# Second-layer products as three partial products for all blocks, fewer working buffers, a shorter weight decode, and values split out of a buffer of their own, in a fused attention and rational feed-forward kernel on one core

## The chip, the core and the metric

The kernel runs on one core of one Trainium2 chip, as one program. The metric is the device time of one execution in microseconds (us), as the median of several runs. The core's engines that matter here are TensorE (PE, with its weight loads as a row of its own, PEld), VectorE (DVE), ScalarE (ACT), GpSimd (POOL, which here only issues transfers and a few tiny instructions) and SyncE (SP, which issues transfers and transposes by DMA). Each engine works through its own list of instructions in order; they meet through semaphores.

## The reference, cut to what matters

```python
# q, k, v: (8 batches, 8 heads, 576 positions, 64) float32; tau a scalar; weights arrive as float64
scores = (1/8) * q @ k^T
scores = where(scores >= max(scores) - tau, scores, -1e9)      # per row
attn   = exp(scores - max) / (sum + 1e-9)
x      = (attn @ v), heads side by side                        # 4608 tokens x 512

h = x @ w_in                                                   # 512 -> 2048
g = (a0 + a1 h + a2 h^2 + a3 h^3) / (1 + |b0| |h| + |b1| h^2 + 1e-6)
out = g @ w_out                                                # 2048 -> 512
```

The result is float32. Products of 16-bit parts and products of shortened 32-bit parts are therefore done as several partial products that are summed in PSUM.

## The kernel before, in words

**Attention.** The eight heads of a batch are worked on as four pairs. A unit is one pair and one tile of 128 queries (four tiles, and a rest of 64 queries), so a batch has 20 units and the program 160. A unit makes scores on PE (`f_qk`), their row maximum on DVE (`f_max`, lines 786 and 788), the threshold and the exponential on ACT (`f_pre` 801, `f_sum` 805), and then, from the second batch on, splits the weights into a high and a low fp16 part: high on ACT or DVE (`f_hi`, through the helper `times`, lines 303 and 305), low on DVE (`f_lo`, 827). The parts are transposed by DMA and multiplied on PE with the values V, which are split in the same way (`f_av`, 896). In the first batch the weights stay float32 ("plain") and V is used unsplit.

**Values before.** There are five V buffers. A pair's V is loaded into one (`load_v_ops`, 659 and 663), the unused corners are cleared by two small `MEMSET`s on DVE (683), its largest absolute value is found, and when all four pairs of the batch have theirs, the batch's scale. Then V is split: the high part into a work buffer `u` (`vh`, through `times`), the low part over the raw values (`vl`, 712), and the high part copied behind it (`vc`, 715).

**Feed-forward blocks.** 256 tokens form a chunk, and a block is one chunk and four of the 16 tiles of hidden units (the last block is cut into two halves: 73 blocks in the trace). A block makes layer 1 on PE (`f_g1`, 1013: 48 products), takes h out of PSUM on ACT (`f_h`, 1022), and then runs a chain over 128x1024 tiles: |h| on ACT or DVE, four multiply-adds on DVE for the two polynomials (1033, 1036, 1046 and, after the quotient, 1055), logarithm and exponential on ACT for the reciprocal (`f_ln` 1040, `f_inv` 1043), one Newton step on DVE (1049, 1052). `box["r"]` is then g. Layer 2 (`f_g2`) multiplies each of the four 128x256 tiles of g by its tile of w_out in two groups, one for each 128 tokens: eight groups per block.

**The two kinds of layer-2 group.** For hidden tiles with an odd number (`in_parts`, `PARTS = 2`), g is rounded to the short fp32r form (`f_gh`, a copy on ACT, line 295, or DVE, line 297) and the remainder is formed on DVE (`f_gl`, 1063); w_out was split once in the same way (`f_wh`, `f_wl`). A group is then three fp32r products (1072). For even tiles a group is one product in full float32 (1076), which the trace shows as two PE instructions.

**Weights.** They arrive as 64-bit floats and are turned into float32 on the chip, 32 tiles of 128x512 (`decode_ops`): the upper word times 2^-112 (`f1`, ACT or DVE), the lower word shifted (`f2`, ACT), the upper word shifted left by 3 (`f4`, DVE), the sign bit put back from the raw word (`f5`, DVE, 479) and the two added (`f6`, DVE). The tiles lie in the buffers `t`, ten of 4 KB per partition, which the feed-forward blocks use too: each block holds one for h, one for q and one for r.

**The order of the work.** Nothing is scheduled on the chip. Python code (`Plan.order`) lists all operations with an assumed duration, a due position (`key`, in units of attention), what they need and which buffers they take and release, and simulates the engines; the order in which it starts operations is the order in which the instructions are written to each engine. Operations with two entries in `FLEX` go to ACT or DVE as the planner finds better. Due positions of the feed-forward blocks come from `SPACE0`, `SPACING`, `ENDK` and `ENDS`, those of the weight tiles from `WHEN`. Transfers of the first eight pairs are issued by SP, later ones and all weights by POOL, in the planner's order; an issue that waits for its buffer holds up those behind it.

## Time and profile before

| | |
|---|---|
| median of 3 runs | 1313.39 us (1311.52 to 1314.45) |
| the profiled execution, its own time | 1315.6 us |
| its span, first to last instruction | 1313.8 us |
| granted TensorE clock, mean | 0.995 |
| PE busy | 1285.3 us, 98% of the span |
| PE weight loads busy | 866.0 us, 66% |
| DVE busy | 1200.6 us, 91% |
| ACT busy | 1064.5 us, 81% |
| POOL busy | 248.0 us, 19% |

Busy time is the time in which an engine had at least one instruction in work. Instructions of one engine overlap a little at their ends, so the sum of the single durations is more than the busy time, and one more instruction costs its engine less than its own duration: the distance from its start to the next start. A row of a timeline names start, duration, engine, line, tiles, shapes and count, and in brackets the idle time ahead of it with what ended it.

### The profile page before, as it was taken

The page shows a single profiled execution, that of the slowest core. Times are in us where ns is not written, and L with a number is a line of the kernel's source. Part 1 is how long each engine was busy: PE and PEld are TensorE (multiplying, and loading weights), DVE is VectorE, ACT ScalarE, POOL GpSimd, SP SyncE. Part 2 cuts the span into 40 slices and gives each one's busy share as a digit, 9 for nine tenths or more (in the row PEclk, how much of TensorE's full clock was granted, in tenths as well). Part 3 has the DMA queues.
Part 4 walks back from the last instruction along what each step waited for, and adds up shares of the span by engine and source line. Part 5 has one row for each costly group of instructions (what it writes and reads, how often), then busy time and mean ns, then how long its engine had stood idle before and what let it go on. Part 6 is the DMA issues. An engine that isn't in the chain of part 4 may idle for free. (4 is left out here: it accounts for less than half of the span.)

```text
span 1313.8 us, 24744 instructions
## 1 busy us (share of the span) xinstructions
PE 1285.3 (98%) x9112; PEld 866.0 (66%) x9112; DVE 1200.6 (91%) x1981; ACT 1064.5 (81%) x2094; POOL 248.0 (19%) x474
## 2 busy tenths in 40 slices
PE   8988999999999999999999999999999999999998
PEld 6666676666666676666667576666667666677775
DVE  6989999999989999999988999999989999897766
ACT  5996989988988897778888798888887878874454
POOL 3211100023122321222111241322032211100000
PEclk9999999999999999999999999999999999999999
DMA  8532435676666664675663765775575746530000
GB/s 248 162 116 81 147 89 105 132 146 133 122 131 119 126 118 101 114 145 115 116 95 77 138 155 108 148 140 117 103 141 111 132 86 116 104 74 1 17 16 17
DMA packets 340585, 146.62 MB, mean 112 GB/s; under 512 B 316208, under 2 KB 323184, under 8 KB 340464
## 3 DMA queue, kind: packets, MB, share of 16 engines
q1 hardware_dynamic: 316400, 86.49, 37.8%
q0 software_dynamic: 22784, 57.31, 15.7%
q8 instruction: 72, 1.18, 0.4%
q10 hardware_dynamic: 1280, 1.25, 0.4%
q14 instruction: 49, 0.40, 0.1%
HBM read 60.30 MB, written 9.44 MB: 53 GB/s over the span
## 5 line engine op out<-in xcount | busy, mean ns | idle before, releaser
L1013 PEld LDWEIGHTS <-wi 128*128 128x128 f16 x3456 | 332.7, 98 | 64.8 <-issue 27.7
L1013 PE MATMUL banks<-x,wi 128*128 128x256 f16 x3072 | 360.2, 273 | 3.7 <-ACT pT L295 1.9
L1076 PE MATMUL banks<-wp,t 128*128 128x512 f32 x576 | 279.8, 601 | 2.3 <-DVE t L1055 2.1
L1072 PE MATMUL banks<-wp,g 128*128 128x512 f32 x864 | 276.4, 451 | 0.7 <-DVE g L1063 0.7
L805 ACT ACTIVATE e<-e,cf 128x576 f32<-128x576 f32 x288 | 221.1, 776 | 0.1
L801 ACT ACTIVATE e<-banks,st 128x576 f32<-128x576 f32 x288 | 206.2, 738 | 17.4 <-DVE st L795 12.0
L1072 PEld LDWEIGHTS banks<-wp,g 128*128 128x128 f32 x864 | 158.6, 189 | 78.5 <-issue 40.0
L827 DVE SCALAR_TENSOR_TENSOR e<-e,st,hi 128x576 f16<-128x576 f32 x252 | 204.2, 810 | 5.5 <-ACT hi L303 3.7
L303 ACT ACTIVATE hi<-e,st 128x576 f16<-128x576 f32 x192 | 144.7, 769 | 52.0 <-DVE st L816 42.3
L786 DVE TENSOR_REDUCE st<-banks 128x2 f32<-128x1152 f32 x128 | 172.3, 1346 | 10.3 <-PE banks L780 9.8
L776 PE MATMUL banks<-KK,QQ 64*128 64x512 f32 x512 | 151.3, 645 | 4.1 <-ACT e L801 3.5
L1076 PEld LDWEIGHTS banks<-wp,t 128*128 128x128 f32 x576 | 101.4, 190 | 74.2 <-issue 60.9
L1022 ACT ACTIVATE t<-banks,hsc 128x512 f32<-128x512 f32 (+1 forms) x192 | 106.4, 576 | 36.4 <-PE banks L1013 35.8
L896 PEld LDWEIGHTS <-V 128*64 128x64 f16 x2520 | 102.9, 111 | 28.9 <-issue 25.7
L896 PE MATMUL banks<-pT,V 128*64 128x256 f16 (+1 forms) x2520 | 121.0, 249 | 0.4 <-DVE V L715 0.4
L1049 DVE SCALAR_TENSOR_TENSOR t<-t,co,t 128x1024 f32<-128x1024 f32 (+1 forms) x73 | 92.2, 1263 | 30.5 <-ACT t L1043 30.5
L1040 ACT ACTIVATE t<-t,co 128x1024 f32<-128x1024 f32 (+1 forms) x73 | 82.6, 1132 | 36.3 <-DVE t L1046 36.2
L780 PEld LDWEIGHTS banks<-KK,QQ 128*128 128x128 f32 x256 | 38.3, 188 | 97.8 <-issue 87.9
L621 POOL DMA_DIRECT2D QQ<-in_qT_dram x42 | 22.4, 533 | 386.0 <-PE banks L767 227.8
L1033 DVE SCALAR_TENSOR_TENSOR t<-t,co 128x1024 f32<-128x1024 f32 (+1 forms) x73 | 92.1, 1262 | 2.2 <-ACT t L1022 2.2
L1055 DVE SCALAR_TENSOR_TENSOR t<-t,co,t 128x1024 f32<-128x1024 f32 (+1 forms) x73 | 92.2, 1264 | 0.8
L1046 DVE SCALAR_TENSOR_TENSOR t<-t,co,t 128x1024 f32<-128x1024 f32 (+1 forms) x73 | 92.1, 1262 | 0.0
(132 smaller groups left out, 1654.2 us busy)
## 6 DMA issues: line engine op xcount, KB each, us to landing
t<-in_w_in_dram POOLq DMA_DIRECT2D x16, 512.0 KB, 5.1
t<-in_w_out_dram POOLq DMA_DIRECT2D x16, 512.0 KB, 5.6
out_dram<-u POOLq DMA_DIRECT2D x26, 256.0 KB, 3.7
V<-in_v_dram POOLq DMA_DIRECT2D x24, 256.0 KB, 4.6
QQ<-in_qT_dram POOLq DMA_DIRECT2D x42, 144.0 KB, 2.8
KK<-in_kT_dram POOLq DMA_DIRECT2D x42, 144.0 KB, 4.0
QQ<-in_qT_dram POOLq DMA_DIRECT2D x42, 128.0 KB, 2.8
KK<-in_kT_dram POOLq DMA_DIRECT2D x42, 128.0 KB, 2.9
```

Of the source, the lines that this page charges most:

```text
L303: nc.scalar.activation(dst, src, AF.Identity, scale=factor)
L776: nc.tensor.matmul(d, QQ[r, t * P:(t + 1) * P], KK[r, REM:S], **one)
L786: nc.vector.tensor_reduce(box["st"][:, 0:2], box["both"], AX.X, ALU.max, negate=True)
L801: nc.scalar.activation(ev(hh), box["s"][hh], AF.Prelu, scale=SCALE, bias=box["st"][:, 2 + hh:3 + hh], alpha=STEEP)
L805: nc.scalar.activation(e, e, AF.Exp, scale=passes, accum_out=box["st"][:, 4 + hh:5 + hh])
L827: nc.vector.scalar_tensor_tensor(box["lo"][:, c], ev(hh), box["st"][:, 6 + hh:7 + hh], box["hi"][:, c], ALU.mult, ALU.subtract)
L896: nc.tensor.matmul(dst, V[:, c * P + hh * D:c * P + (hh + 1) * D], rhs, start=c == 0 and n == 0, stop=c == NT and n == 2)
L1013: nc.tensor.matmul(d, wi_tile(c, f0 + j, hl), x[:, c, :], start=c == 0 and n == 0, stop=c == NC - 1 and n == 2)
L1022: nc.scalar.activation(box["h3"][:, 2 * k:2 * k + 2, sl], psv[:, :, sl], AF.Identity, scale=hsc[:, b2, g:g + 1])
L1049: nc.vector.scalar_tensor_tensor(box["q"], box["q"], qc, box["i"], ALU.add, ALU.mult)
L1072: nc.tensor.matmul(acc[tt], fr(g[:, x]), fr(wo[f][y]), start=begins and j == n == 0, stop=ends and j == nb - 1 and n == 2)
L1076: nc.tensor.matmul(acc[tt], box["r"][:, o:o + P], wo[f], start=begins and j == 0, stop=ends and j == nb - 1)
```

## The change

- **Layer 2.** `PARTS` goes from 2 to 4 and `in_parts` now says yes for every hidden tile. All eight groups of a block are three fp32r products; the full float32 products are gone. So all four tiles of g are rounded (`f_gh`) and their remainders formed (`f_gl`), and all 16 tiles of w_out are split, 8 more than before. The buffers `g` for the parts go from 2 to 3. A block's buffer for r is released when the last remainder is formed, no longer when PE has read it.
- **Buffers.** `t` goes from 10 to 6, `x` (layer 1's input) from 3 to 2.
- **Weight decode.** `f1` is now one ACT instruction (`Prelu` with slope 2^32 for negative values), which carries the sign into the bits that the shift then moves into the sign's place; `f5` is gone, and `f1` no longer runs on DVE.
- **Values.** From the second batch on, raw V goes to a buffer of its own, `VR`, of which there is one. Each pair's V is loaded twice: once for the largest value, and again when it is to be split. The split writes both parts straight into one of now four V buffers, so the copy `vc` and the clearing `MEMSET`s are gone.
- **The planner's numbers** (spacing, prices, tolerances) are changed.

```diff
-POOLS = {"e": 3, "hi": 2, "pT": 2, "st": 8, "sc": 2, "t": 10, "u": 3, "g": 2, "x": 3, "xr": 1}
+POOLS = {"e": 3, "hi": 2, "pT": 2, "st": 8, "sc": 2, "t": 6, "u": 3, "g": 3, "x": 2, "xr": 1}
...
-LEAD, SPACE0, SPACING = 2.3618, 2.8866, 2.0262
-ENDK, ENDS = 6.3041, 10.3733
+LEAD, SPACE0, SPACING = 2.3618, 2.8866, 2.0504
+ENDK, ENDS = 6.3041, 10.4119
...
-NV = 5
+NV = 4
+
+NVR = 1
...
-PARTS = 2
+PARTS = 4
+
+GB = 1
...
     def in_parts(f):
-        return f % PARTS == PARTS - 1
+        return f % NC >= NC - PARTS
...
-            times(box["w"], box["rw"][:, :, 1].bitcast(F32), REBIAS)
+            nc.scalar.activation(box["w"], box["rw"][:, :, 1].bitcast(F32), AF.Prelu, scale=REBIAS, alpha=SIGN)
...
-        def f5():
-            t = box["w"].bitcast(I32)
-            nc.vector.scalar_tensor_tensor(t, box["rw"][:, :, 1], -0x80000000, t, ALU.bitwise_and, ALU.bitwise_or)
...
-        o1 = op(FLEX["f1"], 0, key, f1, [l], [ht])
+        o1 = op("ACT", 0.567, key, f1, [l], [ht])
...
-        o5 = op("DVE", 0.602, key, f5, [o4])
-        o6 = op(FLEX["f6"], 0, key, f6, [o5, o2], (), [ht] if dst is None else [ht, hold])
+        o6 = op(FLEX["f6"], 0, key, f6, [o4, o2], (), [ht] if dst is None else [ht, hold])
...
+        raw, vhold = Hold("vr", 2), Hold("v", NT // 2 + 1)
+        vh_[bp] = vhold
+        l = load_v(bp, p - V2, raw)

         def vh():
-            times(high(), Vs[vh_[bp].slot], sx[:, bb:bb + 1])
+            times(v_part(vhold.slot, 1), v_raw(raw), sx[:, bb:bb + 1])

         def vl():
-            t = Vs[vh_[bp].slot]
-            nc.vector.scalar_tensor_tensor(v_part(vh_[bp].slot, 0), t, sx[:, bb:bb + 1], high(), ALU.mult, ALU.subtract)
-
-        def vc():
-            nc.vector.tensor_copy(v_part(vh_[bp].slot, 1), high())
-        o = op(FLEX["vh"], 0, p, vh, [isx_done[bb]], [vhi])
-        v_ops[bp] = p, o, vl, vc, vhi
+            nc.vector.scalar_tensor_tensor(v_part(vhold.slot, 0), v_raw(raw), sx[:, bb:bb + 1], v_part(vhold.slot, 1),
+                                           ALU.mult, ALU.subtract)
+        o = op(FLEX["vh"], 0, p, vh, [isx_done[bb], l], [vhold], [raw])
+        v_done[bp] = op(FLEX["vl"], 0, p + 0.1, vl, [o], (), [raw])
...
-        hh, hq, hr = Hold("t", 1), Hold("t", 1), Hold("t", 2 * nb)
+        hh, hq, hr = Hold("t", 1), Hold("t", 1), Hold("t", 2 * len(runs) + 2 * (nb - len(js)))
```

**What moves, at three places.** First, DVE in the tail, after the last attention unit, where only feed-forward blocks are left: one period of a block. The lines are 1033, 1036, 1046, 1049, 1052, 1055 for the chain, 297 for a rounding of g on DVE and 1063 for a remainder. Before:

```order
L1033 SCALAR_TENSOR_TENSOR t_76<-t_72,co 128x1024
L1036 SCALAR_TENSOR_TENSOR t_77<-t_77,co 128x1024
L1046 SCALAR_TENSOR_TENSOR t_76<-t_76,co,t_72 128x1024
L1049 SCALAR_TENSOR_TENSOR t_77<-t_77,co,t_72 128x1024
L1052 SCALAR_TENSOR_TENSOR t_77<-t_77,t_72 128x1024
L1055 SCALAR_TENSOR_TENSOR t_76<-t_76,co,t_77 128x1024
L297 CAST g_99<-t_76 128x256
L1063 TENSOR_TENSOR g_99<-t_76,g_99 128x256
L1063 TENSOR_TENSOR g_98<-t_76,g_98 128x256
```

In the changed kernel the same chain stands on lines 1020, 1023, 1033, 1036, 1039, 1042, and the remainder on 1055:

```order
L1020 SCALAR_TENSOR_TENSOR t_68<-t_70,co 128x1024
L1055 TENSOR_TENSOR g_94<-t_69,g_94 128x256
L1055 TENSOR_TENSOR g_95<-t_69,g_95 128x256
L1055 TENSOR_TENSOR g_96<-t_69,g_96 128x256
L1023 SCALAR_TENSOR_TENSOR t_73<-t_73,co 128x1024
L1033 SCALAR_TENSOR_TENSOR t_68<-t_68,co,t_70 128x1024
L1055 TENSOR_TENSOR g_94<-t_69,g_94 128x256
L1036 SCALAR_TENSOR_TENSOR t_73<-t_73,co,t_70 128x1024
L1039 SCALAR_TENSOR_TENSOR t_73<-t_73,t_70 128x1024
L1042 SCALAR_TENSOR_TENSOR t_68<-t_68,co,t_73 128x1024
```

Three of the four remainders now stand behind the next block's first multiply-add, the fourth behind its third, where DVE otherwise waits for logarithm and exponential; the roundings are on ACT here.

Second, DVE at the start of the program, the decode of the first weight tiles (475 or 480 is the shift, 479 the sign, 310 or 315 the sum). Before, and then in the changed kernel:

```order
L305 TENSOR_SCALAR u_78<-t_68 128x512
L475 TENSOR_SCALAR u_78<-u_78 128x512
L479 SCALAR_TENSOR_TENSOR u_78<-t_68,u_78 128x512
L310 ISA t_68<-t_68,u_78 128x512x2
L786 TENSOR_REDUCE st_90<-banks 128x2
```

```order
L480 TENSOR_SCALAR u_74<-u_74 128x512
L774 TENSOR_REDUCE st_86<-banks 128x2
L315 ISA t_68<-t_68,u_74 128x512x2
L800 TENSOR_SCALAR st_84<-st_84 128x2
L480 TENSOR_SCALAR u_75<-u_75 128x512
```

Of four DVE instructions for a tile two are left.

Third, POOL's list of transfers in a batch of the middle (Q 621 to 623, K 628 to 633, V 659 and 663 before; Q 622 to 624, K 629 to 634, V 682 and 686 after). Before:

```order
L630 DMA KK_118<-in_kT_dram 64x64
L633 DMA KK_118<-in_kT_dram 64x64 x2
L659 DMA V_162<-in_v_dram 128x4x128
L663 DMA V_162<-in_v_dram 64x64 x2
L621 DMA QQ_115<-in_qT_dram 64x576
```

```order
L1088 DMA out_dram<-u_76 128x512
L682 DMA VR_169<-in_v_dram 128x4x128
L686 DMA VR_169<-in_v_dram 64x64 x2
L682 DMA VR_169<-in_v_dram 128x4x128
L686 DMA VR_169<-in_v_dram 64x64 x2
L622 DMA QQ_112<-in_qT_dram 64x576
```

The changed list has 48 loads of V where it had 24 (with two corner loads each), all but the first batch's into the one buffer VR, and the next pair's Q and K stand behind them.

Counted over the whole program, per engine: PE loses 288 float32 groups and gains 288 groups of three fp32r products. DVE: remainders of g (1063) 144 to 288, roundings of g (297) 60 to 94, sign operations (479) 32 to 0, rebias (305, `u<-t`) 22 to 0, V copies (715) 28 to 0, V clears (683) 54 to 0, high parts of attention weights (305, `hi`) 60 to 41, w_out remainders (567) 8 to 16. ACT: roundings of g (295) 84 to 194, rebias (303, `u<-t`, now `Prelu`) 10 to 32, high parts (303, `hi`) 192 to 211, w_out roundings (295) 5 to 11. By stages, and by the place in DVE's list (first batch; batches two to seven; from the eighth on): remainders of g 4, 98, 42 before and 8, 200, 80 after; sign operations 29, 3, 0 before; blocks finished (1055) 2, 49, 22 before and 2, 50, 21 after.

More of the change, by code (lines that the diff above doesn't have):

```diff
@@ L687, in load_v_ops @@
-        if pr == NP - 1:
-            isx_done[bb] = scale_ops(p if bb else 4.0, lambda: vms[bb], 14, isx[:, bb:bb + 1], sx[:, bb:bb + 1], vm_ops[bb])
-            for i in range(NP):
-                split_v_ops(bb * NP + i)
-            if bb == 0:
-                isx_done["up"] = op("DVE", 0.12, 4.0, lambda: nc.vector.tensor_scalar(sxu, sx[:, 0:1], UP, None, ALU.mult), [isx_done[0]])
+        return op(eng, 1.6, key, ld, (), [hold])
     def split_v_ops(bp):
         bb, pr = divmod(bp, NP)
-        later = [pos[bp, t] for t in range(NT + 1) if not is_plain(bp, t)]
@@ L1069, in f_g2 @@
             if in_parts(f):
-                g = box["g", j][:, :, tt * P:(tt + 1) * P]
+                o = (j - runs[run[j]][0]) * CT + tt * P
+                g = box["g", run[j]][:, :, o:o + P]
                 for n, (x, y) in enumerate(((0, 0), (1, 0), (0, 1))):
```

132 lines of the change are left out of this document (67 added, 65 removed).

## The prediction

> **What bounds the kernel now.** I read the page's busy shares first, then a table by stage, and then timelines in the tail, because a share over the whole span mixes stages.
>
> ```profile
> PE 1285.3 (98%) x9112; PEld 866.0 (66%) x9112; DVE 1200.6 (91%) x1981; ACT 1064.5 (81%) x2094; POOL 248.0 (19%) x474
> ...
> core 0: us, PE busy (x) PEld busy (x) DVE busy (x) ACT busy (x) POOL busy (x), PEclk, DMA share, GB/s
> 0.00:158.30 158.30, 143.31 (x950) 101.44 (x950) 136.19 (x331) 126.37 (x280) 28.93 (x70) 0.96 0.52 154
> 158.30:1021.00 862.70, 857.04 (x6272) 568.86 (x6271) 823.98 (x1328) 740.97 (x1457) 195.70 (x360) 1.00 0.63 121
> 1021.00:1164.90 143.90, 141.72 (x1037) 94.11 (x1036) 132.00 (x202) 124.26 (x241) 22.20 (x42) 1.00 0.55 103
> 1164.90:1313.80 148.90, 143.24 (x860) 101.59 (x857) 108.41 (x126) 72.85 (x118) 1.12 (x2) 1.00 0.08 21
> ```
>
> The stages are cut where DVE starts the row maximum of the first unit of the second and of the eighth batch, and where it ends the last one: the **head** (first batch, weight decode), the **middle** (six batches), the **last batch**, and the **tail** (feed-forward blocks only). In the middle PE is busy for 99.3%, DVE for 95.5%, ACT for 86%: PE is the bound, with DVE four points behind. In the head no engine is full over the whole stage. One batch shows how densely DVE can be packed here:
>
> ```profile
> 158.30:303.80 145.50, 142.69 (x1060) 96.57 (x1059) 142.19 (x245) 129.45 (x253) 15.99 (x28) 1.00 0.58 119
> ```
>
> 142.19 of 145.50 us is 97.7%. That number decides the middle, below.
>
> In the tail PE repeats one period; the columns are start, duration, engine, line, operation:
>
> ```profile
> 1203.71 1.88 PE L1076 MATMUL banks<-wp,t 128*128 128x512 f32 x4
> 1205.03 1.96 PE L1072 MATMUL banks<-wp,g 128*128 128x512 f32 x6
> ...
> 1209.95 5.42 PE L1013 MATMUL banks<-x,wi 128*128 128x256 f16 x48
> 1215.20 1.88 PE L1076 MATMUL banks<-wp,t 128*128 128x512 f32 x4
> ...
> 1204.14 1.45 PE L1076 MATMUL banks<-wp,t 128*128 128x512 f32 x3
> ...
> 1205.66 0.62 PE L1072 MATMUL banks<-wp,g 128*128 128x512 f32 x2
> ...
> 1205.89 0.39 PE L1072 MATMUL banks<-wp,g 128*128 128x512 f32 x1
> ```
>
> A block takes 1215.20 - 1203.71 = 11.49 us of PE. Starts inside a run give the price of one group: float32 steps by 0.43 (1203.71 to 1204.14), two per group, 0.86 us; fp32r steps by 0.23 (1205.66 to 1205.89), three per group, 0.70 us. Four of each are 6.24 us, which is the distance from 1203.71 to 1209.95. The gap is 0.16 us per group.
>
> **PE's term.** 288 groups x 0.16 = 46 us less PE work: 0.64 us per block of four changed groups. Everything else asks what stops PE from using it.
>
> **What an added instruction costs DVE and ACT.** From the groups by line, and from a pair of neighbours:
>
> ```profile
> L1063 DVE TENSOR_TENSOR g<-t,g 128x256 fp32r<-128x256 f32 x144 | 55.8, 417 | 1.2 <-ACT g L295 0.9
> L295 ACT CAST g<-t 128x256 fp32r<-128x256 f32 x84 | 31.9, 399 | 19.6 <-DVE t L1055 19.2
> L297 DVE CAST g<-t 128x256 fp32r<-128x256 f32 x60 | 16.3, 289 | 1.0
> L479 DVE SCALAR_TENSOR_TENSOR u<-t,u 128x512 int32<-128x512 int32 x32 | 21.7, 685 | 0.2
> L305 DVE TENSOR_SCALAR u<-t 128x512 f32<-128x512 f32 x22 | 9.1, 421 | 0.2
> L715 DVE COPY V<-u 128x640 f16<-128x640 f16 x28 | 8.4, 318 | 0.0
> L683 DVE MEMSET V<- 64x64 f32 x54 | 6.0, 112 | 1.4
> L305 DVE TENSOR_SCALAR hi<-e,st 128x576 f16<-128x576 f32 x60 | 30.7, 518 | 0.7
> L303 ACT ACTIVATE u<-t 128x512 f32<-128x512 f32 x10 | 6.8, 681 | 4.2 <-DMA t<-in_w_in_dram 2.2 <-PE banks L408 2.0
> ...
> 1203.46 0.76 DVE L1063 TENSOR_TENSOR g<-t,g 128x256 fp32r<-128x256 f32 x2
> 1204.13 1.28 DVE L1033 SCALAR_TENSOR_TENSOR t<-t,co 128x1024 f32<-128x1024 f32 x1
> 1205.33 1.28 DVE L1036 SCALAR_TENSOR_TENSOR t<-t,co 128x1024 f32<-128x1024 f32 x1
> ```
>
> Two remainders of 0.417 us take 0.67 until the next start, and a 1.28 us instruction 1.20: each costs its duration less 0.08 us. On ACT I subtract 0.1 (an estimate from the busy time of line 295, 31.9 us for 84, and its mean). With the counts by stage in the order of instructions:
>
> - *Head.* DVE loses 29 sign operations (29 x 0.60 = 17.4) and about 22 rebias operations and others of their kind with 26 x 0.34 = 8.8, and gains six w_out remainders (3.6), four g remainders (1.3) and three maxima of V (2.2), less small things: -23 us, 136.2 to 113. ACT gains 28 rebias operations (16) less 11 scalings of the same shape (7), four w_out roundings and two |h|: +14 us, 126.4 to 140.6.
> - *Middle.* DVE gains 102 remainders x 0.335 = 34.2, 20 roundings x 0.21 = 4.1, eight chain steps of a further block and a half x 1.2 = 9.6, and some 8 in splits of V that move in and scale operations; it loses 24 copies x 0.24 = 5.7, 48 clears (about 7), 17 high parts that go to ACT x 0.43 = 7.3, and the last three sign operations (1.8). Sum +36: 824.0 to 859.7 us. ACT gains 82 roundings x 0.3 = 25, 17 high parts x 0.67 = 11, and some 12 more: 741 to about 790.
> - *Last batch and tail.* DVE's additions (38 remainders, 13 roundings: 15 us) and one block fewer cancel: 240.4 to 240.
>
> So the saving of 46 us on PE is bought with 13 us on DVE and some 60 on ACT, and DVE's part falls on the middle, where it is four points from full.
>
> **The sum, stage by stage.**
>
> *Head, 158.3 to 155 us.* DVE's relief is real, but ACT takes its place: it cannot begin before the first maximum,
>
> ```profile
> 11.40 1.37 ACT L801 ACTIVATE e<-banks,st 128x576 f32<-128x576 f32 x2 [9.38 <-DVE st L795]
> ```
>
> at 11.4 us, and 140.6 us at 98% density end at 155. If it is filled no better than DVE was (136.2 over 148.6 us, 92%) the head ends at 164; if the order leaves room for DVE's relief, at 148.
>
> *Middle, 862.7 to 877 us.* PE needs some 17 us less (49 blocks x 0.64 = 31, less one and a bit of 11 us added); DVE, with 859.7, becomes the bound. At 98%, just above the batch quoted, in which PE was still full beside it, the stage lasts 859.7 / 0.98 = 877. Bounds: 868 at 99%, 900 at today's 95.5%.
>
> *Last batch and tail, 292.8 to 271 us.* In the last batch PE is full and eight blocks save 8 x 0.64 = 5. The tail has 13 blocks for 14: -11.5. The others do not save all 0.64, because DVE's own period binds next:
>
> ```profile
> 1199.16 1.28 DVE L1049 SCALAR_TENSOR_TENSOR t<-t,co,t 128x1024 f32<-128x1024 f32 x1 [2.37 <-ACT t L1043]
> 1203.13 0.29 DVE L297 CAST g<-t 128x256 fp32r<-128x256 f32 x1
> 1206.53 1.28 DVE L1046 SCALAR_TENSOR_TENSOR t<-t,co,t 128x1024 f32<-128x1024 f32 x1
> 1210.17 1.28 DVE L1049 SCALAR_TENSOR_TENSOR t<-t,co,t 128x1024 f32<-128x1024 f32 x1 [2.37 <-ACT t L1043]
> ```
>
> Where DVE does not wait for PE its period is 1210.17 - 1199.16 = 11.01 us, with 2.37 of it waiting for logarithm and exponential. The changed order puts three remainders (1.0) where a rounding and two remainders stood (1.0), and the fourth inside that wait, so the period stays 11.0, above PE's 10.85. 13 x (11.49 - 11.01) = 6.2. At the end one more rounding and remainder stand ahead of the last products, +1. Sum -22: 271.
>
> *Span* 155 + 877 + 271 = 1303 us. The profiled execution's own time is 1.8 above its span, and 2.2 above the median of the runs (1315.6 against 1313.39), so **1302.6 us** for the median, 0.8% less.
>
> **Edits costed at nothing.** The second load of V (28 x one 256 KB transfer and two corners) is read only by the split, whose due place is two units (some 14 us) ahead of its first product; a landing takes
>
> ```profile
> t<-in_w_in_dram POOLq DMA_DIRECT2D x16, 512.0 KB, 5.1
> ...
> V<-in_v_dram POOLq DMA_DIRECT2D x24, 256.0 KB, 4.6
> ...
> POOL V L659 <- PE banks L896: 181.8, 18, 19.6
> POOL t L513 <- DVE wi L537: 20.7, 2, 15.2
> ...
> DVE t L1049 <- ACT t L1043: 30.5, 16, 4.0
> ```
>
> 4.6 us. POOL's long waits for a V buffer (181.8 us, for PE to finish reading) end with VR, whose readers are ACT and DVE; what queues behind a late VR are the next pair's Q and K, needed four units later. Without that cover a pair would cost up to 4.6 us, 28 of them 129. Six `t` buffers hold two feed-forward blocks of three; a third block at once is needed only when a block stays over two spacings (862.7 / 49 = 17.6 us each in the middle). In the head weight loads wait for a `t` buffer already with ten (20.7 us at line 513, behind line 537): see the rivals. The third `g` buffer and the second `x` I take as free: PE reads them in list order.
>
> A row and a rule that speak against the change: `L683`, `L715` leave DVE, but 72 more transfers are issued by POOL, each as long as this row, while DVE's remainders show a narrow spread (shortest, median, longest ns):
>
> ```profile
> L663 POOL DMA_DIRECT2D V<-in_v_dram x48 | 25.2, 531 | 2.5 <-issue 2.5
> ...
> L1063 DVE TENSOR_TENSOR g<-t,g x144: 400/417/427, 111.8 to 1305.5; 128x256 fp32r<-128x256 f32 x144
> ```
>
> The Trainium skill (SBUF — State Buffer, "Who interferes with whom") says that GpSimd and some VectorE instructions take turns on one pair of SBUF ports, and the later one waits for the whole of the other. By that rule the 34 added roundings on DVE and POOL's issues would stretch each other; in this trace the spread of 27 ns over 144 instructions shows no such wait.
>
> **Rivals.**
>
> 1. *DVE packs to 99% and the head follows DVE.* 148 + 868 + 271 = 1287, 1286.6 as a median. For it: ACT is 86% busy in the middle, and V's clears, which wait for a transfer, are gone. Against: ACT rises to 90%.
> 2. *DVE gets no denser in the middle* (the other side): it stays at 95.5% because its idle time is the wait for ScalarE in the chain (line 1049 after 1043, 30.5 us in all), which ACT's extra 50 us lengthen. 155 + 900 + 271 = 1326, 1325.6. It decides below 859.7 / 887.8 = 96.8%, where the total is today's. For it: that wait, and every block now has two engines' hops more between g and PE. Against: the batch at 97.7%. By the Trainium skill (Perfetto Trace Analysis, "Identifying the Most-Contended Engine") matmul busy time is no measure of PE's limit and the share of weight loads is a better one; that is 66% here, which would make DVE the bound already and favour this rival. The tail's starts, back to back at 11.49 us, speak for PE.
> 3. *Six `t` buffers starve the decode in the head.* If each of the four groups of weights waits one landing more (5.1 us, the row above for w_in) the head is 20 us longer: 1322.6.
> 4. *Port turns on POOL's issues*: 72 x 0.531 = 38 us on DVE in the middle, 1341.
> 5. *The three products are no cheaper inside the middle*: PE gives nothing, DVE costs 13: about 1327.
>
> **How the numbers follow.** Forecast 0.47, rivals 0.27, 0.16, 0.06, 0.01, 0.03. About 0.2% (1310.8 to 1316.0) is what a measurement here tells from no change. The forecast's own range is 1292 (head 148, middle 873) to 1313 (head 164, middle 878); I give it 0.42 faster, 0.04 same, 0.01 slower. With rival 1: 0.69 faster; 0.08 same, with a mild form of rivals 2 and 3; 0.23 slower. The range reaches from 1282 to 1324: it holds rival 1, rival 3 and the near half of rival 2.
>
> **What would show it.** Lines 1065 (products) with a 0.23 step everywhere and PE's work about 46 us less; in the middle DVE at or above 97.5% and PE near 96%; a tail period of 11.0 us with DVE waiting about 2.4 us at line 1036 for 1030; in the head ACT at 19 of 20 us in most slices. Wrong would be: DVE below 96.8% in the middle; PE weight loads waiting for V or K; POOL waiting for `t` for much more than 20 us at one place in the head with PE idle behind it.

## The result, and the profile after

The changed kernel takes **1319.54 us** (median of five runs, 1317.99 to 1322.84), the kernel before 1313.39 (1311.52 to 1314.45): a ratio of 1.0052, 95% interval 1.0034 to 1.0069. It is slower by some 6 us, where 1302.6 and "faster" had been forecast.

The page of the changed kernel, its busy row and four of its groups (busy us, mean ns, idle before and its releaser):

```profile
PE 1261.5 (96%) x9462; PEld 932.5 (71%) x9462; DVE 1209.0 (92%) x2004; ACT 1115.3 (85%) x2258; POOL 285.4 (22%) x536
...
L1065 PE MATMUL banks<-wp,g 128*128 128x512 f32 x1728 | 447.0, 405 | 7.8 <-DVE g L1055 4.3
...
L1055 DVE TENSOR_TENSOR g<-t,g 128x256 fp32r<-128x256 f32 x288 | 109.8, 415 | 8.6 <-ACT g L300 8.5
...
L1036 DVE SCALAR_TENSOR_TENSOR t<-t,co,t 128x1024 f32<-128x1024 f32 (+1 forms) x73 | 92.2, 1262 | 16.4 <-ACT t L1030 16.0
...
L682 POOL DMA_DIRECT2D VR<-in_v_dram x48 | 38.1, 794 | 251.0 <-DVE V L702 100.7
```

The engines' sums came near what was reckoned: 8 us more on DVE (13 forecast) and 51 more on ACT (some 60), and the full float32 products are gone (1728 products on line 1065 in place of 864 and 576). PE's busy time fell by 24 us only, half of the 46 us of work that left it. The same four stages, cut at the same maxima (columns as before: length, then busy time of PE, PEld, DVE, ACT, POOL):

```profile
0.00:167.30 167.30, 145.98 (x952) 104.25 (x953) 115.65 (x272) 138.97 (x307) 21.25 (x57) 0.92 0.47 139
167.30:1055.30 888.00, 860.58 (x6647) 630.56 (x6647) 857.63 (x1382) 784.30 (x1587) 240.59 (x435) 0.99 0.64 128
1055.30:1186.40 131.10, 130.95 (x1035) 96.09 (x1034) 128.20 (x210) 118.01 (x233) 23.11 (x44) 1.00 0.62 116
1186.40:1317.10 130.70, 124.02 (x833) 101.58 (x830) 107.53 (x142) 74.01 (x136) 0.42 (x1) 1.00 0.10 23
```

| stage | before | forecast | after |
|---|---|---|---|
| head | 158.3 | 155 | 167.3 |
| middle | 862.7 | 877 | 888.0 |
| last batch and tail | 292.8 | 271 | 261.8 |
| span | 1313.8 | 1303 | 1317.1 |

The last two stages won 31 us, 9 more than forecast; the head lost 9 and the middle 25. In the middle DVE's busy time is 857.6 us, 2 us from the forecast's 859.7, at 96.6% of the stage and not the 98% assumed. PE has room: its idle time there rose from 6 to 27 us. The first two of the six batches of the middle (the second row stands for most of the others):

```profile
167.33:319.84 152.51, 141.78 (x1114) 104.44 (x1113) 142.45 (x243) 131.72 (x268) 23.07 (x40) 0.98 0.60 129
319.84:466.73 146.89, 143.88 (x1102) 105.70 (x1101) 143.86 (x232) 128.09 (x258) 41.07 (x76) 1.00 0.65 130
```

In four of the six batches DVE is busy for 97.3 to 97.9%, as dense as the forecast had it within a point. In the first it is at 93.4%, with PE at 93.0% beside it, and in the fourth at 95.8%. At 98% throughout, DVE's 857.7 us would have lasted 875; of the 12.8 us above that, these two batches hold 10.7. (The profiled execution before lay 2.2 us above its median, the one after 0.7 below, which is why the spans differ by 3.3 us and the medians by 6.2.)

### The profile page after: what moved, and what is told of

It reads as the page before. It is cut to its first block, busy times and chain, and to the rows that moved or that the text cites. A ratio compares the mean times of both kernels' runs of the same rounds, so it can differ in the third digit from the quotient of the medians.

```text
span 1317.1 us, 25798 instructions
## 1 busy us (share of the span) xinstructions
PE 1261.5 (96%) x9462; PEld 932.5 (71%) x9462; DVE 1209.0 (92%) x2004; ACT 1115.3 (85%) x2258; POOL 285.4 (22%) x536
## 4 chain that ended last, share of the span: by engine, by line
PE 30%; DVE 27%; issue 8%; ACT 8%; DMA 5%; POOL 2%; DVEq 0%; ACTq 0%; POOLq 0%
PE banks L1065 13%; PE banks L1000 9%; DVE e L815 5%; DMA VR<-in_v_dram 4%; DVE st L774 3%; PE banks L884 3%; PE banks L764 3%; DVE t L1036 2%; DVE g L1055 2%; DVE t L1020 2%; DVE t L1039 2%; DVE t L1023 2%; DVE t L1033 2%; DVE t L1042 2%; ACT e L793 1%
## 5 line engine op out<-in xcount | busy, mean ns | idle before, releaser
L1065 PE MATMUL banks<-wp,g 128*128 128x512 f32 x1728 | 447.0, 405 | 7.8 <-DVE g L1055 4.3
L1000 PE MATMUL banks<-x,wi 128*128 128x256 f16 x3072 | 364.9, 275 | 15.2 <-ACT t L1009 9.1
L1065 PEld LDWEIGHTS banks<-wp,g 128*128 128x128 f32 x1728 | 314.1, 189 | 84.5 <-DVE g L1055 11.0
L308 ACT ACTIVATE hi<-e,st 128x576 f16<-128x576 f32 x211 | 160.8, 770 | 47.1 <-DVE st L804 42.0
L1055 DVE TENSOR_TENSOR g<-t,g 128x256 fp32r<-128x256 f32 x288 | 109.8, 415 | 8.6 <-ACT g L300 8.5
L300 ACT CAST g<-t 128x256 fp32r<-128x256 f32 x194 | 72.7, 399 | 36.3 <-PE banks L1065 16.4
L682 POOL DMA_DIRECT2D VR<-in_v_dram x48 | 38.1, 794 | 251.0 <-DVE V L702 100.7
```

What stands on the lines that cost most here:

```text
L308: nc.scalar.activation(dst, src, AF.Identity, scale=factor)
L1000: nc.tensor.matmul(d, wi_tile(c, f0 + j, hl), x[:, c, :], start=c == 0 and n == 0, stop=c == NC - 1 and n == 2)
L1055: nc.vector.tensor_tensor(fr(g[:, 1]), box["r"][:, r[0] * CT:(r[-1] + 1) * CT], g[:, 0], ALU.subtract)
L1065: nc.tensor.matmul(acc[tt], fr(g[:, x]), fr(wo[f][y]), start=begins and j == n == 0, stop=ends and j == nb - 1 and n == 2)
```

## Experiments with parts of the change, each with a new order

Theories at that point, by the letters used below: **T**, six `t` buffers hold up decode and blocks; **D**, VectorE's added work; **V**, the single buffer of raw V; **C**, PE's clock, which falls after gaps; **S**, the scatter of the order, in which any edit that the planner sees gives another list.

### Ten `t` buffers in the changed kernel, and six in the kernel before

```diff
-POOLS = {... "t": 6, ...}                      # e1, changed kernel
+POOLS = {... "t": 10, ...}
-        wo[f] = [wpool.tile(...) for i in range(2)]
+        wo[f] = wo[f - 1] if f % 2 else [wpool.tile(...) for i in range(2)]
-POOLS = {... "t": 10, ...}                     # e2, kernel before
+POOLS = {... "t": 6, ...}
```

> The changed kernel with ten t buffers again. To make room, each pair of neighbouring hidden tiles shares one split tile of w_out, so the second layer multiplies by the wrong weights for half of its tiles; every load, decode step, split and product is still there in number and shape. Theory T (six t buffers hold up the weight loads in the head, and a third feed-forward block in the middle): the head ends at about 155 to 158 us instead of 167, the middle shrinks from 888 to about 875, the time is about 1297 to 1305 us. Theory D (VectorE's added remainders and roundings fill it in the middle, whatever the buffers): 1316 to 1321 us, head and middle as in the changed kernel.

> The kernel before with six t buffers instead of ten and nothing else. Theory T: slower by 10 to 20 us, 1323 to 1333, the head 9 us or more longer, the last weight tile loaded some 50 us later. Theory D: within 3 us of 1313.

Measured: e1 1325.7 us (ratio to the kernel before 1.0103, 1.0069 to 1.0136), head 165.6, middle 893.9. The buffers given back bring nothing in the total. e2 1345.6 us (1.0254, 1.0231 to 1.0277): with six buffers and a new list the kernel before is 32 us longer. The two do not fit one theory of buffers.

### All groups in parts alone, and half of them

```diff
-        return f % PARTS == PARTS - 1           # e3, kernel before; w_out tiles shared as in e1, "g": 3
+        return True
-        return f % NC >= NC - PARTS             # e4, changed kernel
+        return f % 2 == 1
```

> The kernel before with all groups of the second layer as three partial products and three g buffers, still ten t buffers, old decode, old path of V. Neighbouring hidden tiles share one split tile of w_out as in the first of these runs, so half of the second layer multiplies by the wrong weights. Theory T: the 46 us of TensorE pay in part, 1300 to 1308 us. Theory D: VectorE has some 60 us more work and nothing taken away, 1320 to 1335 us, VectorE at 97% in the middle.

> The changed kernel with half of the hidden tiles as full float32 products again, as before (every second one); six t buffers, new decode, new path of V kept. Theory T: the head as in the changed kernel (165 to 169), TensorE back at 99% in the middle, 1322 to 1335 us. Theory D: VectorE is relieved, 1300 to 1313 us.

Measured: e3 1337.8 us (1.0187, 1.0145 to 1.0228); e4 1348.5 (1.0276, 1.0236 to 1.0317). Read alone, the first says that parts for all groups cost 24 us, the second that giving half of them up costs 29 more. Both cannot be the price of that edit.

### Two buffers for raw V, PE kept warm, and the planner's numbers exchanged

```diff
-NVR = 1                                         # e5
+NVR = 2
-WARM, WARM_END = 0.6, 400.0                     # e6
+WARM, WARM_END = 0.9, 1300.0
-SPACING = 2.0504 ...                            # e7, changed kernel: SPACING, ENDS, WHEN, V1, AHEAD_RANK,
+SPACING = 2.0262 ...                            #     EARLY, EARLY_END, PRICE, TOL of the kernel before
                                                 # e8: the kernel before with those of the changed one
```

> The changed kernel with two raw V buffers instead of one. Theory V (the one buffer VR chains load, read, load, and late V hold up ScalarE and VectorE): POOL's waits at the VR load fall from some 200 us to under 100, ScalarE and VectorE lose their 20 us of waits on VR, the time falls by 5 to 12 us to 1307 to 1314. Theory C (TensorE's granted clock drops after its idle gaps, mostly in the head): no change beyond 4 us. Theory S (scatter of the planner's list order): a change of up to 10 us either way, without the VR waits explaining it.

> The changed kernel with more filling products on TensorE: 90% of each planned idle gap instead of 60%, and over the whole program instead of the first 400 us of the plan. Theory C: the clock lost (span times one less the granted clock) falls from 18.7 us to under 10, the head from 167 to under 162, the time to 1308 to 1314. Theory V and theory D (VectorE full in the middle): 1316 to 1323.

> The changed kernel with the planner's numbers (spacings, due places, prices, tolerances) of the kernel before. No instruction is added or removed but those that go from ScalarE to VectorE or back. Theory S: 10 to 30 us slower, by denser or looser lists and more idle gaps on TensorE, which says that a part of the change can't be judged without its own numbers. Theories D, V and C: within 6 us of the changed kernel.

> The kernel before with the planner's numbers of the changed kernel. Theory S: 10 to 30 us slower than 1313. Theories D, V and C: within 6 us of 1313.

Measured: e5 1344.1 us (1.0233), e7 1352.7 (1.0297), e8 1344.5 (1.0234), each with intervals of about 0.004 to either side. Changing nothing but the planner's numbers costs either kernel 31 to 33 us (e7, e8). That is **S**: a new list with numbers that do not belong to it costs five times the difference in question. The four runs that changed something else as well and were planned anew (e2, e3, e4, e5) are 24 to 33 us longer than the kernel they were made from, which is the same size, so they price no part of the change. That e1 lies only 6 us off the changed kernel says as little: as a time it tells neither for T nor against it.

e6 is the exception: it keeps the list and only adds fill-in products on PE. 1321.8 us (1.0066, 1.0038 to 1.0093), although PE's clock was better. Two stretches of the head, of the changed kernel and of e6 (the eighth column is PE's granted clock):

```profile
100.00:110.00 10.00, 5.55 (x37) 4.24 (x36) 6.59 (x9) 6.34 (x17) 1.68 (x3) 0.78 0.78 216
110.00:120.00 10.00, 10.00 (x48) 6.95 (x46) 5.62 (x13) 7.98 (x22) 0.53 (x1) 0.88 0.18 56
```

```profile
100.00:110.00 10.00, 6.59 (x41) 4.71 (x42) 7.55 (x15) 7.46 (x20) 1.16 (x2) 0.83 0.77 220
110.00:120.00 10.00, 10.00 (x58) 7.45 (x56) 4.73 (x11) 8.82 (x22) 0.53 (x1) 1.00 0.18 54
```

A better clock for PE brought no time in the total (mean 0.989 for 0.986). That is not C alone: the head is 2.8 us shorter (164.5), the middle 4.0 longer (892.0), and there the fill-in itself adds 11.9 us to PE's busy time. So C as the cause of the whole difference is not borne out; a few us of the head may be its.

## Experiments with the order kept

From here on the list of work was left exactly as the planner had made it, and only what an operation writes to its engine was changed. The stage cuts stay comparable. A run's stages are those of its one profiled execution, which lay up to 5.4 us above the median of its run (e12) and up to 3.8 below (e11), so a stage that moves by 3 or 4 us has not surely moved. One correction to the expectations of e10, e12, e13 and e15: a remainder serves two token halves, so the products left out or added are 288, not 144, and PE's work moves by 288 x 0.233 = 67 us (some 45 of them in the middle), twice what stands there.

### Less work on one engine: e9, e10, e12

```diff
         def f_gl(k):                            # e9, changed kernel
             r, g = runs[k], box["g", k]
+            if k % 2 == 0:
+                return
...
-for n, (x, y) in enumerate(((0, 0), (1, 0), (0, 1))):                # e10, changed kernel
+for n, (x, y) in enumerate(((0, 0), (1, 0), (0, 1))[:2 + j % 2]):
...
-for n, (x, y) in enumerate(((0, 0), (1, 0), (0, 1))):                # e12, kernel before
+for n, (x, y) in enumerate(((0, 0), (1, 0))):
```

> The changed kernel with its list of work exactly as it is; of the remainders that VectorE makes of the activations those of every second hidden tile are not issued (144 of 288; g is cleared once at the start, so a part of the second layer's sum is left out). VectorE has 144 x 0.335 = 48 us less work, about 34 of them in the middle, and nothing else moves. Theory D (VectorE's sum of work sets the middle, and 96.6 % is as dense as this list lets it be): the middle falls until TensorE stops it, from 888 to about 867 (860.6 us of products at 99.3 %), the head by some 3, the tail by some 2, the whole to about 1294. Theory W (the middle is made of scattered waits along the list, in which no engine's sum decides): 5 to 10 us at most, 1310 to 1315.

> The changed kernel with its list of work exactly as it is; of the three products of a group the third (rounded activation by remainder of the weight) is left out in every second hidden tile, 144 of 864 products, 144 x 0.233 = 33.6 us of TensorE, about 24 of them in the middle. Theory D: the middle stays (0 to -4 us), the last batch, where TensorE is full for 130.95 of 131.1 us, gains up to 4, the tail at most 2: 1310 to 1319. If TensorE still binds in the middle: about -30, 1290. Theory W: about half of it, 1300 to 1306.

> The kernel before with its list of work exactly as it is; in the 144 groups made of parts the third product is left out, 144 x 0.233 = 33.6 us of TensorE, about 24 of them in the middle. This asks the step on which the forecast rested, whether VectorE packs denser when TensorE gives way. If it does, to 98 %: the middle falls from 862.7 to about 841, the last batch by 4 and the tail by some 6 (to VectorE's period of 11.0), the whole by about 30, to 1283. If 95.5 % is what this list lets VectorE be: the middle falls by 0 to 5, the whole by 8 to 14, to 1300 to 1305.

Measured: e9 1308.7 us (0.9968, 0.9953 to 0.9983), e10 1315.0 (1.0010, 0.9996 to 1.0023), e12 1301.8 (0.9902, 0.9884 to 0.9920). The middle of e12, then of e9, then of e10:

```profile
159.05:1018.19 859.14, 830.39 (x6080) 539.87 (x6079) 822.55 (x1328) 737.83 (x1457) 195.17 (x360) 1.00 0.64 121
```

```profile
165.59:1050.30 884.71, 860.18 (x6647) 631.77 (x6646) 831.50 (x1283) 783.42 (x1588) 240.01 (x435) 0.99 0.64 129
```

```profile
161.60:1050.52 888.92, 833.99 (x6450) 600.27 (x6449) 857.28 (x1383) 782.56 (x1588) 241.38 (x435) 0.99 0.65 128
```

e12 asks the forecast's step directly. In the kernel before, PE's busy time in the middle fell by 26.7 us, from 99.3% to 96.7% of the stage, and the stage by 3.6 (at most some 7, if all that its profiled execution lay above the median belongs here): DVE went from 95.5% to 95.7%, not to 98%. In the changed kernel the same cut on PE gains nothing in the middle (888.0 to 888.9), and 26 us less on DVE gain 3.3.

### Less on both: e13

```diff
+the edits of e9 and e10 together
```

> The changed kernel with its list of work exactly as it is, with the cuts of the two runs before it together: in every second hidden tile neither the remainder (144 x 0.335 = 48 us of VectorE) nor the third product (33.6 us of TensorE) is issued. Alone they moved the whole by -10.9 and -4.5 us and the middle by -3.3 and +0.9. Theory K (TensorE and VectorE take turns at being last along one list, so that relief of one is taken up by the other): together far more than the sum, the middle -12 to -25, the whole 1288 to 1298. Theory L (waits and latencies along the list, which neither engine's work decides): the sum of the two, the middle about 885, the whole about 1304.

Measured: **1287.0 us** (0.9803, 0.9777 to 0.9829), 32.5 under the changed kernel, where the two alone gave 10.8 and 4.5. Its middle:

```profile
161.16:1037.21 876.05, 830.06 (x6448) 600.27 (x6446) 829.02 (x1283) 780.21 (x1586) 240.55 (x435) 0.99 0.66 130
```

888.0 to 876.1, where the singles moved it by -3.3 and +0.9; the last batch and the tail lost 5.6 and 5.4, alone at most 1.7. This is what theory K expects: PE and DVE take turns at being last along one list, and relief of one alone is taken up by the other. It is not all there is: some 30 us less on each gave 12 in the middle, and the middle's first batch, 152.5 us in the changed kernel, did not move at all (152.1 in e9, 152.6 in e13).

### More work on one engine, in the kernel before: e14, e15, e16

```diff
+            nc.vector.tensor_tensor(fr(g[:, 1]), box["r"][...], g[:, 0], ALU.subtract)   # e14: made twice
-for n, (x, y) in enumerate(((0, 0), (1, 0), (0, 1))):                                    # e15
+for n, (x, y) in enumerate(((0, 0), (1, 0), (0, 1), (1, 1))):
+            nc.scalar.copy(spare, box["r"][:, j * CT:(j + 1) * CT])                      # e16
```

> The kernel before with its list of work exactly as it is, each of its 144 remainders made twice: 144 x 0.335 = 48 us more on VectorE, about 34 in the middle, which is what the change adds there (33.7). Theory K: most of it is paid, the middle +22 to +34, the whole +30 to +48, 1343 to 1361. Theory L: VectorE's 38.7 us of idle time in the middle take most of it in, the whole +5 to +15, 1318 to 1328.

> The kernel before with its list of work exactly as it is, a fourth product (remainder by remainder) in each of its 144 groups in parts: 144 x 0.233 = 33.6 us more on TensorE, about 24 in the middle. If TensorE binds there, as the forecast read from 99.3 %: the middle +22 to +27, the tail +13, the whole about +33, 1346. If its busy time only fills what the others leave, as the cut in this kernel says (26.7 us less busy time, 3.6 us gained): the middle +4 to +10, the whole +12 to +20, 1325 to 1333.

> The kernel before with its list of work exactly as it is, beside each of its 144 roundings of activations one more copy of the same 128x256 on ScalarE to a place that nobody reads: 144 x 0.3 = 43 us, about 31 in the middle, where the change adds 43 to ScalarE. ScalarE is 86 % busy there. If idle time takes it in: the whole within +5, 1313 to 1318. If ScalarE's place in the chains counts (theory L): +12 to +25, 1325 to 1338.

Measured: e14 1362.9 us (1.0387, 1.0360 to 1.0414), e15 1374.1 (1.0468, 1.0444 to 1.0493), e16 1322.0 (1.0081, 1.0053 to 1.0108), between its two expectations. Their middles, in this order:

```profile
158.79:1054.81 896.02, 874.57 (x6274) 574.73 (x6273) 863.80 (x1426) 739.34 (x1457) 195.61 (x360) 1.00 0.61 116
```

```profile
159.48:1062.70 903.22, 898.82 (x6466) 604.88 (x6465) 829.87 (x1328) 745.91 (x1458) 195.85 (x360) 1.00 0.60 115
```

```profile
159.54:1025.43 865.89, 858.86 (x6272) 570.16 (x6271) 824.88 (x1329) 768.34 (x1555) 195.36 (x360) 1.00 0.64 120
```

This gives a price list for the middle of the kernel before (862.7 us; busy 857.1, 824.0 and 741.0):

| run | work changed (busy us) | stage (us) | price per us |
|---|---|---|---|
| e15 | PE +41.7 | +40.5 | 0.97 |
| e14 | DVE +39.8 | +33.3 | 0.84 |
| e16 | ACT +27.4 | +3.2 | 0.12 |
| e12 | PE -26.7 | -3.6 | 0.13 |

Added work on PE and on DVE is paid nearly in full, though DVE seemed to have 38.7 us of idle time; work removed from PE alone is worth an eighth of it (a quarter at most, with the 7 us above). The prices hold for this list, and for work added where these runs added it.

### The second load of V: e11, e18

```diff
-        l = load_v(bp, p - V2, raw)             # e11, changed kernel
+        l = op("DMA" if bp < EARLY_BP else "GD", 1.6, p - V2, lambda: None, (), [raw])
...
-    Vrs = [const.tile(...) for i in range(NVR)]                       # e18, changed kernel
+    Vrs = [const.tile(...) for i in range(2)]
+            if hold.pool == "vr":
+                hold.raw = Vrs[turn[0] % 2]; turn[0] += 1
```

> The changed kernel with its list of work exactly as it is; the second load of each pair's V, which the split reads, is not issued (28 transfers of 256 KB and 56 corners less; the split takes what stands in the buffer, so the values are left wrong). Theory V (the waits for that load and for its one buffer put the execution behind its list): the middle falls by the 5.5 us that VectorE and some of the 13.8 us that ScalarE wait for it, to 870 to 880, the whole to 1302 to 1312. Theory D or W without V: within 3 us of the changed kernel, 1317 to 1322.

> The changed kernel with its list of work exactly as it is; the transfers into the one buffer of raw V go to two places in turn, so that a load need not wait until the transfer before it has been read. Leaving the load out gave 8 us. If those are the waits for the buffer (GpSimd waits 251 us for it in all): most of the 8 back, 1311 to 1315, as fast as the kernel before. If they are the landing of a load that is issued in time but used at once: 0 to 2 us, 1317 to 1320.

Measured: e11 1311.6 us (0.9978, 0.9962 to 0.9994), e18 1321.2 (1.0052, 1.0030 to 1.0074). Leaving the load out gives 8 us, a second buffer nothing, though GpSimd's largest group of waits for the buffer fell from 100.7 to 31.1 us in total. These are the three largest waits of POOL in the changed kernel, and then two rows of e18 (total, times, longest):

```profile
POOL QQ L622 <- PE banks L755: 183.3, 18, 34.1
POOL QQ L622 <- PE banks L768: 101.8, 16, 13.7
POOL VR L682 <- DVE V L702: 100.7, 14, 18.3
```

```profile
POOL QQ L623 <- PE banks L759: 290.5, 22, 34.1
...
POOL VR L686 <- DVE V L706: 31.1, 5, 8.6
```

What POOL no longer waits at VR it waits at the next load of Q, whose buffer PE still reads; all these issues stand in one queue. That V's loads are late because they stand behind Q's fits this, but no run with another order of the issues was made, so it is not shown. In the middle of the changed kernel the readers wait for VR here; lines 310 and 308 are the split, which reads the second load (7.7 us), lines 659 and 661 the largest value, which reads the first:

```profile
DVE V L310 <- DMA VR<-in_v_dram: 3.3, 3, 1.9
DVE vm L659 <- DMA VR<-in_v_dram: 2.2, 2, 1.4
...
ACT u L661 <- DMA VR<-in_v_dram: 9.4, 6, 3.3
ACT V L308 <- DMA VR<-in_v_dram: 4.4, 5, 3.0
```

### The decode alone, in the kernel before: e17

```diff
-            times(box["w"], box["rw"][:, :, 1].bitcast(F32), REBIAS)
+            nc.scalar.activation(box["w"], box["rw"][:, :, 1].bitcast(F32), AF.Prelu, scale=REBIAS, alpha=SIGN)
...
-            nc.vector.scalar_tensor_tensor(t, box["rw"][:, :, 1], -0x80000000, t, ALU.bitwise_and, ALU.bitwise_or)
+            return
```

> The kernel before with its list of work exactly as it is; only the decode is the changed one: the rebias is one ScalarE operation that keeps the sign, and the sign operation on VectorE is not issued. VectorE loses 32 x 0.60 + 22 x 0.34 = 26.7 us, nearly all in the head, ScalarE gains 22 x 0.57 = 12.5. The forecast's step for the head (VectorE's relief is real, ScalarE takes its place): 158.3 to 155, the whole about 1310. If the decode edit itself is what made the changed head 9 us longer (ScalarE late for the first units): the head 162 to 168, the whole 1317 to 1323. If only both engines' relief together is worth anything, as in the middle: within 2 us of the kernel before.

Measured: **1320.8 us** (1.0059, 1.0043 to 1.0076), as slow as the whole change. Its head, and the largest wait of DVE there:

```profile
0.00:164.93 164.93, 145.99 (x948) 102.75 (x949) 114.31 (x284) 136.31 (x299) 26.71 (x70) 0.95 0.50 148
```

```profile
DVE u L475 <- ACT u L468: 11.8, 12, 2.5
```

DVE has 21.9 us less to do, ACT 9.9 more, and the head is 6.6 us longer. DVE now waits for the rebias (line 475 for line 468, twelve times), of which it used to make 22 of 32 itself. In the head of the changed kernel the same pair of lines stands with seven waits:

```profile
DVE u L480 <- ACT u L473: 7.1, 7, 1.8
```

In this list, which was planned for the old decode, ACT's added work costs the head more than DVE's relief brings.

## Why the prediction was wrong, point by point

**"PE is the bound, with DVE four points behind"**: the first step that failed. PE was a bound (e15: 0.97 per us added), but so was DVE (e14: 0.84), and it did not pack denser when PE alone stepped back (e12: 95.7%). Of DVE's 38.7 us of idle time little was room in that list (e14 found some 7 us); it is waits in the chains that the list leaves, the softmax first. DVE's two largest in the middle of the kernel before:

```profile
DVE st L816 <- ACT st L810: 9.6, 7, 2.6
DVE st L812 <- ACT e L805: 8.6, 12, 1.8
```

An engine's share shows how much it waits, not whether work can be put there.

The forecast weighed the Trainium skill's rule (Perfetto Trace Analysis, "Identifying the Most-Contended Engine") that matmul busy time is no good measure of how near PE is to its limit. e12 agrees as far as it goes: some 45 us less of matmul work (192 products of 0.233) took 26.7 us off the busy time and 3.6 off the stage. By the section DVE, at 95.5% of the middle against 66% for PE's weight loads, would be the one engine to relieve first; that is not what e15 and e9 show: both engines bind.

**"At 98% the stage lasts 877"**: the second step. DVE's sum was right (857.6 for 859.7; the items as the prediction lists them add up to +34, not the +36 that it wrote, and +33.6 came); the density fell short, 96.6% against a break-even of 96.8% as the prediction worked it out. By batches it came within a point in four of six, so the 97.7% batch was a fair measure of what a list can give. What the forecast missed is the first batch, where both engines idle, and in part the fourth. In the first, the `t` buffers, whose number was costed at nothing there, run short:

```profile
180.22 0.53 POOL L552 DMA_DIRECT2D t<-in_w_out_dram  x1 [30.70 <-DVE wi L537]
...
200.85 0.68 DVE L567 TENSOR_TENSOR wp<-t,wp 128x512 fp32r<-128x512 f32 x1
...
201.65 1.26 ACT L1009 ACTIVATE t<-banks,hsc 128x512 f32<-128x512 f32 x2 [3.57 <-DVE wp L567]
...
202.39 6.83 PE L1000 MATMUL banks<-x,wi 128*128 128x256 f16 x36 [5.21 <-ACT t L1009]
```

GpSimd waits 30.7 us, mostly in the head, to load a tile of w_out into a `t` buffer; the last such load is issued at 191.8 us, where it was 139.0 before. ACT (line 1009) takes h out of PSUM into a `t` buffer and waits for line 567, which reads one and writes nothing that line 1009 reads: what it lacks is the buffer. PE waits for ACT, and its 36 products after the gap take 0.190 us each for 0.113 in the tail (granted clock 0.59). That is some 8 us of PE's time at one place (an estimate: 5.2 + 36 x 0.077). The kernel before has no such wait, nor has e1 with ten buffers, whose last w_out load is issued at 174.6. How much of it is the six buffers and how much the planner's new due places was not measured with the order kept. V's loads are the other part that is seen there: without the second one (e11) the batch lasts 148.0 us for 152.5.

So the middle lies between the forecast's 877 and the 900 of rival 2 ("DVE gets no denser"). The wait that rival 2 gave as its reason is not in the middle: of the 30.5 us that line 1049 waits for 1043 before, 0.9 lie there and 27.3 in the tail (2.0 and 13.6 of 16.0 now, lines 1036 and 1030). The price list of the kernel before would give 33.6 x 0.84 + 43.3 x 0.12 less some 17 us of PE's work x 0.13, that is 28 + 5 - 2 = 31 us; 25.3 were measured. That is near, but it does not show that DVE's work made the 25: with 26 of the 34 us taken off again (e9) the middle is still 22 us longer than before.

**"Head, 158.3 to 155"**: the third step, and with 12.3 us the largest miss of a stage (the middle missed by 11.0). That ACT takes DVE's place was right (139.0 us busy for 140.6 forecast), that it packs at 98% was not: from its first work at 11.4 us it is busy for 88% of the head, less than even the 92% of the forecast's bound. The decode edit alone makes the head of the kernel before 6.6 us longer and its median 8.3 (e17), in a list that was not planned for it. In the changed kernel with its list kept (e9, e10, e11, e13, e18) the head lasts 161.2 to 165.6 us, though little of these edits falls there, so a part of the 9 may be the scatter of single executions. How much is decode, buffers, clock (below) or order stays open.

**"Last batch and tail, 292.8 to 271"**: right in kind, undersized by 9, of which the tail is 1.5 (130.7 for 132.2). The tail, PE and DVE of the changed kernel:

```profile
1236.09 5.84 PE L1065 MATMUL banks<-wp,g 128*128 128x512 f32 x24
1241.77 5.42 PE L1000 MATMUL banks<-x,wi 128*128 128x256 f16 x48
1246.94 5.85 PE L1065 MATMUL banks<-wp,g 128*128 128x512 f32 x24
```

```profile
1241.10 1.28 DVE L1036 SCALAR_TENSOR_TENSOR t<-t,co,t 128x1024 f32<-128x1024 f32 x1 [1.98 <-ACT t L1030]
...
1251.86 1.28 DVE L1036 SCALAR_TENSOR_TENSOR t<-t,co,t 128x1024 f32<-128x1024 f32 x1 [1.97 <-ACT t L1030]
```

A block takes 1246.94 - 1236.09 = 10.85 us, PE's own period as worked out, and DVE follows at 10.76: its wait shrank from 2.37 to 1.97 us, so the 11.0 at which the forecast let DVE bind did not hold. The price of a product held: 24 from 1236.09 to 1241.77 are 0.237 each, for 0.233. The last batch gave 12.8 us where 5 were expected (143.9 to 131.1). Eight blocks end in it in both kernels and should bring it 32 PE instructions more, but their number went from 1037 to 1035: some work of that batch now stands elsewhere, and the saving there is not all cheaper products.

**V's second load "costed at nothing"**: wrong by some 8 us (e11). The cover named was two units; the split waits for it all the same. The prediction priced the lack of cover at 4.6 us a pair, 129 in all; the runs say 0.3 a pair.

**Rivals 3, 4 and 5**: rival 3, six `t` buffers, happened in part: POOL's wait of 30.7 us and PE's of 5.2 above are close to the sign that the prediction named, though PE's falls at the start of the middle. POOL's waits at `t` are 150 us in all, 84 before; what they cost the head is not shown (e1 with ten buffers left it long, 165.6 for 167.3, in another list). Port turns: the remainders last 415 ns on average after and 417 before, the roundings 287 and 289, so POOL's 62 more instructions do not stretch them. Three products are cheaper, as the tail shows.

**What paid for what.** Span: head +9.0, middle +25.3, last batch and tail -31.0, sum +3.3. The saving of PE's work arrived where PE alone set the pace, at the end. In the middle, where two thirds of the blocks lie (49 of 73), PE and DVE both bind, so PE's saving could win little there (e12: 0.13 per us, a quarter at most). That the stage lost 25 us is accounted for only in part: 7.2 us go with V's second load (e11) and some 8 of PE's time with the `t` buffer, two sums that may overlap; what the rest owes to DVE's 34 us and to the new list is not shown.

## What to carry to other kernels

When two engines are above 95% in a stage, price a change by adding work and by taking it away on each, with the order kept: here the two prices of PE differed by a factor of four to seven, so an edit that trades work of the one for work of the other can lose there even where the trade looks good. Look at the stage batch by batch before calling its mean a limit: here more than half of the missing density lay in one batch of six. Where a planner makes the order, an experiment that lets it plan again measures the new list (here 31 to 33 us with nothing else changed) and not the edit. And idle time of an engine becomes room only if the waits that make it are named and shown to go away.

## What the runs showed of the hardware that was not expected

PE's clock halves for a few us after a gap even in a kernel that is 96% busy. In the head of the changed kernel PE waited 4.45 us, and 24 products took nearly what 48 take in the tail (5.42 us); the granted clock in these 5.27 us was 0.51, and 1.00 in the 5.4 us after them:

```profile
107.33 5.27 PE L1000 MATMUL banks<-x,wi 128*128 128x256 f16 x24 [4.45 <-ACT pT L300]
```

The Trainium skill (TensorE: Matmul & The Clock Gate, the table of the two clock states) has the clock drop to half after an idle window of about 3.4 us; this row agrees. The mean granted clock was 0.986 after, 0.995 before. The lost clock follows from waits; in e6 it was smaller and the time was not.

PE's busy time is elastic: with the same products, work added on DVE took it from 857.1 to 874.6 us in the middle (e14), leaving out a load of V took it from 860.6 to 854.8 (e11), and 197 products of 0.233 us, 46 us of work, took off only 26.6 (e10).
